# Three expert tiles instead of two from the routing of six batches, and the first one's layer 1 in four blocks between the steps of the last router

## The chip, the cores and the metric

The kernel runs on one NeuronCore of a Trainium2 chip: TensorE (PE; its weight loads are PEld), VectorE (DVE), ScalarE (ACT), GpSimd (POOL), the queues of the DMA engines, most of them fed by SyncE (SP), SBUF, and eight PSUM banks. The metric is device time in microseconds, the median of several runs. Every number of the profile comes from one profiled execution.

## The reference

Eight batches, eight heads, 1152 keys of 64 values. Queries are averaged in pairs, so each head has 576. After attention every one of the 8 x 576 = 4608 rows (512 values) goes to one of eight experts:

```python
q_pool = q.reshape(B, H, S // 2, 2, D).mean(axis=3)
attn = softmax(q_pool @ k.transpose(0, 1, 3, 2) / sqrt(D))
x = (attn @ v).transpose(0, 2, 1, 3).reshape(B * 576, 512)
logits = x @ w_gate                                  # 8 experts
e = argmax(logits, axis=1); gate = softmax(logits)[e]
eom = sigmoid(x @ w_output_gate)[e]
out = gate * eom * (relu(x @ w1[e]) @ w2[e])         # 512 -> 1024 -> 512
```

All is float32, and the kernel keeps that precision by splitting operands in a high and a low part.

## The kernel before, in words

**Attention.** The 32 pairs (batch, two heads) go through one software pipeline, written out by hand: 18 steps a pair (two heads, nine blocks of 128 keys), 576 steps and 14 more to empty it. In each step `sgen` issues the score products of one block (L395, L397) into one of two score areas of PSUM (`sps0`, `sps1`, two banks each), ACT makes the exponentials, and their low part `pl` comes from POOL (L411) or, in six steps of 18, from DVE (L405). `mgen` works a pair ahead on row maxima: products into one of three banks (`mp0` to `mp2`, handed out by `psum()`; `psum(True)` keeps a bank until `free`), and a DVE maximum of each (L333). `agen` runs six steps behind with P·V (L426 to L428), in bursts. `prep` loads and splits the next pairs.

**Router.** When a batch's four pairs are done, `logits` and `router` run as generators, moved on by one `yield` a step: transposes of the rows `xb` (L481), products with the gates (L498), sums in `lT` (L502), transposes of `lT` (L523), a chain of small DVE operations, and a product with a triangle (L555 to L558) that ranks each row within its expert. `cum` holds the counts so far. Five indirect DMAs from POOL write the row numbers to the list `idscr`, and the rows go to `xrows` in DRAM.

**Early experts.** After the sixth batch `setup` runs as part of that generator. It takes the counts of six batches, picks the expert with the most rows, takes 256 away, and picks again (so P1 = 2 tiles of 256 rows are full for certain before all is routed). It keeps its scratch in a held PSUM bank. Then `gather_ids` fetches both tiles' row numbers and `gather` the rows of the first.

**Expert tiles.** `Moe.run` handles two early tiles (t = -2, -1) and slots of 13 tiles of 256 rows, four of 192 and three of 128, whose experts and lists come from tables that DVE computes at run time (`totals1`, `totals2`, `table`, `fill`). For a tile, `xt` transposes the gathered rows and splits them into X; `l1` makes layer 1 in four blocks g (16 products each, L944), ACT and DVE add the parts and apply relu (`hs`, `hh`, `hl`); `l2` makes layer 2 for 128 rows at a time (L985 to L988). `split1` and `split2` make high and low parts of the weights: ACT casts, and DVE or POOL subtracts. Weights lie in two buffers, a and b, and `loads(t+2)` fills the one just used up. `gid` and `gat` gather a later tile's row numbers and rows; results are scattered to the output.

**Order at the join.** Orders of TensorE, DVE and ACT are written out within attention (there POOL too) and within the tiles; between these two, and for POOL and SP in the tiles, a scheduler with simulated times decides. `issue_after` and the list `behind` add pure order: in the kernel before, the transposes of tile -2 are pulled forward into the last P·V steps, block g = 0 of its layer 1 goes between the `lT` transposes and the rank product of the last router, and blocks 1 to 3 come after the rank product. SBUF is a stack: a tile of the expert part lies where one of attention lay, and waits for that one's last use.

## Time and profile before

| | us |
|---|---|
| median of three runs | 1492.92 |
| lowest and highest | 1492.88, 1496.63 |
| profiled execution | 1494.86 |
| its span | 1493.1 |
| granted TensorE clock, mean | 0.997 |
| DVE, ACT, POOL busy | 1104.3, 1124.7, 1025.1 |
| last score product starts | 1002.8 |
| last layer-2 product ends | 1486.7 |

Busy time of an engine counts its instructions, not its waits for semaphores. In a row of the time order, the number in brackets is the idle time before it, and the name behind the arrow is what ended it. In a row of the windows, each engine has its busy time and, in brackets, its instructions. Attention fills the first 1008 us, the expert tiles the rest.

### The profile page before, as it was taken

What the parts mean: (1) busy time and instruction counts of PE and PEld (TensorE: products, weight loads), DVE (VectorE), ACT (ScalarE), POOL (GpSimd) and SP (SyncE); (2) the same over time, 40 slices, a digit from 0 to 9 for tenths busy, and PEclk for the clock granted to TensorE, in tenths of its full rate; (3) what the DMA queues carried; (4) which work ended last, traced back from release to release, by engine and by line L of the source; (5) the groups of instructions that cost most, each with busy time, mean ns of one, the idle gap of its engine ahead of it and who ended that gap; (6) DMA issues with size and microseconds to landing.
All of it is one profiled execution on the core that took longest, in us unless ns stands there. A gap on an engine that the chain in (4) does not pass through costs nothing.

```text
span 1493.1 us, 40870 instructions
## 1 busy us (share of the span) xinstructions
PE 1461.7 (98%) x15806; PEld 1330.7 (89%) x15806; DVE 1104.3 (74%) x2374; ACT 1124.7 (75%) x1957; POOL 1025.1 (69%) x900
## 2 busy tenths in 40 slices
PE   7999999999999999999999999999999999999998
PEld 6999999999999999999999899987888888888985
DVE  7677777777777777777777777748888778777863
ACT  6888888888888888888888788884656556556662
POOL 5887889789889879888988898886533323333420
PEclk9999999999999999999999999999999999999999
DMA  5577567656567457755766555444966666666751
GB/s 172 147 179 193 134 157 175 169 136 166 146 163 189 124 137 170 177 148 130 178 168 162 152 136 146 112 147 136 374 244 232 232 240 213 240 234 231 263 211 63
DMA packets 96708, 265.97 MB, mean 178 GB/s; under 512 B 12826, under 2 KB 17066, under 8 KB 96498
## 3 DMA queue, kind: packets, MB, share of 16 engines
q1 hardware_dynamic: 85994, 241.52, 56.0%
q0 software_dynamic: 9088, 20.86, 4.0%
q8 instruction: 129, 2.11, 0.6%
q10 hardware_dynamic: 1424, 0.88, 0.2%
q14 instruction: 73, 0.60, 0.1%
HBM read 160.04 MB, written 22.50 MB: 122 GB/s over the span
## 4 chain that ended last, share of the span: by engine, by line
PE 92%; DVE 4%; DMA 1%; ACT 1%; issue 1%; POOL 1%; ACTq 0%; POOLq 0%; SPq 0%; DVEq 0%
PE mp L332 21%; PE hps L944 15%; PE sps L395 12%; PE sps L397 10%; PE av L426 6%; PE av L427 6%; PE av L428 6%; PE yp L985 4%; PE yp L986 4%; PE yp L988 4%; DVE pm L333 1%; PE tp L481 1%; PE tp L498 1%; PE xps L924 1%; PE yp L983 1%
## 5 line engine op out<-in xcount | busy, mean ns | idle before, releaser
L333 DVE TENSOR_REDUCE pm<-mp 128x1 f32<-128x384 f32 x864 | 452.8, 550 | 210.3 <-PE mp L332 209.5
L411 POOL TENSOR_TENSOR pl<-p,ph 128x576 f16<-128x576 f32 x386 | 493.8, 1285 | 135.0 <-ACT ph L410 103.4
L409 ACT ACTIVATE p<-sps 128x576 f32<-128x576 f32 x386 | 253.0, 655 | 88.7 <-PE sps L397 66.1
L332 PE MATMUL mp<-ka,qa 128*128 128x384 f32 x960 | 314.5, 344 | 0.8 <-DVE lT L502 0.6
L426 PEld LDWEIGHTS <-ph 128*128 128x128 f16 x2880 | 261.9, 96 | 39.4 <-issue 27.7
L426 PE MATMUL av<-vt,ph 128*128 128x65 f16 x2880 | 294.3, 193 | 0.0
L427 PE MATMUL av<-vt,ph 128*128 128x64 f16 x2880 | 292.3, 194 | 0.0
L428 PE MATMUL av<-vt,pl 128*128 128x65 f16 x2880 | 291.5, 192 | 0.0
L395 PE MATMUL sps<-qa,ka 128*128 128x288 f32 x1152 | 276.6, 321 | 4.3 <-DVE pl L405 3.4
L427 PEld LDWEIGHTS <-ph 128*128 128x128 f16 x2880 | 264.7, 97 | 0.8
L428 PEld LDWEIGHTS <-pl 128*128 128x128 f16 x2880 | 265.0, 99 | 0.0
L332 PE MATMUL mp<-kb,qb 66*128 66x384 f32 x768 | 260.4, 339 | 0.6 <-DVE kb L206 0.6
L410 ACT ACTIVATE ph<-sps 128x576 f16<-128x576 f32 x386 | 251.0, 650 | 0.0
L397 PE MATMUL sps<-qb,kb 68*128 68x288 f32 x1152 | 246.4, 296 | 1.0 <-DMA qb<-mr 1.0
L944 PE MATMUL hps<-x,w1h 128*128 128x512 f32 (+2 forms) x704 | 224.4, 382 | 0.6 <-DVE x L931 0.6
L395 PEld LDWEIGHTS sps<-qa,ka 128*128 128x128 f32 x1152 | 183.1, 190 | 7.3 <-DVE pl L405 1.9
L397 PEld LDWEIGHTS sps<-qb,kb 68*128 68x128 f32 x1152 | 185.0, 189 | 1.3 <-issue 1.2
L332 PEld LDWEIGHTS mp<-ka,qa 128*128 128x128 f32 x960 | 178.0, 190 | 3.1 <-DVE pm L333 2.0
L944 PE MATMUL hps<-x,w1l 128*128 128x256 f32 (+2 forms) x704 | 162.8, 272 | 0.0
L957 ACT COPY hs<-hps 128x512 f32<-128x512 f32 (+2 forms) x88 | 47.4, 539 | 147.9 <-PE hps L944 147.8
L405 DVE TENSOR_TENSOR pl<-sps,ph 128x576 f16<-128x576 f32 x190 | 143.6, 756 | 15.8 <-ACT sps L402 14.8
L401 ACT ACTIVATE ph<-sps 128x576 f16<-128x576 f32 x190 | 124.6, 656 | 38.1 <-PE sps L397 30.2
(271 smaller groups left out, 2948.1 us busy)
## 6 DMA issues: line engine op xcount, KB each, us to landing
ka<-xk SPq DMA_DIRECT2D x120, 288.0 KB
raw1a<-in_w_dram SPq DMA_DIRECT2D x22, 1024.0 KB
raw2a<-in_w_dram SPq DMA_DIRECT2D x22, 1024.0 KB
raw1b<-in_w_dram SPq DMA_DIRECT2D x22, 1024.0 KB
raw2b<-in_w_dram SPq DMA_DIRECT2D x22, 1024.0 KB
vp<-in_vL_dram SPq DMA_DIRECT2D x32, 576.0 KB
qp<-in_qT_dram SPq DMA_DIRECT2D x31, 576.0 KB
kpf<-in_kT_dram SPq DMA_DIRECT2D x31, 576.0 KB
```

The source lines that it names most:

```text
L332: nc.tensor.matmul(mp, lhsT=l, rhs=r, start=j == 0, stop=j == len(ops) - 1)
L333: nc.vector.tensor_reduce(out=pm[:, i:i + 1], in_=mp, axis=AX.X, op=ALU.max)
L395: nc.tensor.matmul(sps[:, j, 0:288], lhsT=ka[:, h, ks], rhs=qa[:, o + 288 * j:o + 288 * j + 288], start=True, stop=False)
L397: nc.tensor.matmul(sps[:, j, 0:288], lhsT=kb[:, h, ks], rhs=qb[:, h, 288 * j:288 * j + 288], start=False, stop=True)
L405: nc.vector.tensor_tensor(out=pl.rearrange("p (j n) -> p j n", j=2), in0=x, in1=ph2, op=ALU.subtract)
L409: nc.scalar.activation(out=p32.rearrange("p (j n) -> p j n", j=2), in_=x, func=AF.Exp, scale=1.0 / 16)
L410: e_ = nc.scalar.activation(out=ph2, in_=x, func=AF.Exp, scale=1.0 / 16)
L411: nc.gpsimd.tensor_tensor(out=pl, in0=p32, in1=ph, op=ALU.subtract)
L426: nc.tensor.matmul(av_[:, qb, 0:65], lhsT=hi, rhs=vt[:, h, c, 0:65], start=c == 0 and qb == 0, stop=False)
L427: nc.tensor.matmul(av_[:, qb, 0:64], lhsT=hi, rhs=vt[:, h, c, 66:130], start=False, stop=False)
L428: nc.tensor.matmul(av_[:, qb, 0:65], lhsT=lo, rhs=vt[:, h, c, 0:65], start=False, stop=c == NC - 1 and qb == 4)
L944: d['mm'] = nc.tensor.matmul(hp[:, f, 0:n], lhsT=W1[l][g][:, c, fs], rhs=d['x'][:, c, 0:n], start=c == 0 and l == 0, stop=c == 3 and l == 0)
```

## The change

P1 becomes 3, the slots of 256 rows 12, and tiles are numbered from -3. `setup` copies the counts out of PSUM at once, keeps its scratch in SBUF, and writes its scalar steps as `scalar_tensor_tensor` with a constant one; its gathers are issued one at a time, with three steps between them. The rows of tile -2 are gathered into a pool of their own (`me`), those of -1 into the common one. The stack has a new order: `vt` and `junk` get a pool of their own (`a_v`), X0 and the layer-1 sums (`mh`) move behind the low part of `w2`. The transposes of the first tile go before the first P·V product of the emptying steps (hook `pv`) and use the other score area, with one cast and one subtraction for all of X. Its layer 1 is cut into four blocks that stand behind the last P·V product, the last transposes of `xb`, the transposes of `lT` and the rank products; the hooks `xb`, `logit`, `rank` hold the router's next step back until a block is issued, `lg` and `r1` do the same on DVE with the block's sum. The first two parts of its `w2` are subtracted on POOL. The totals come after block four, and the tables are made in steps (`chain`) during tile -2; the third early tile's weights are loaded without a table.

```diff
-SLOTS = dict(D=13, T=4, S=3)
+SLOTS = dict(D=12, T=4, S=3)
 WIDTH = dict(D=256, T=192, S=128)
-DRAINS = (8, 17)
+DRAINS = (7, 16)
...
+        vp_ = pool("a_v", 1)
...
-                    nc.tensor.matmul(av_[:, qb, 0:65], lhsT=hi, rhs=vt[:, h, c, 0:65], start=c == 0 and qb == 0, stop=False)
+                    t_ = nc.tensor.matmul(av_[:, qb, 0:65], lhsT=hi, rhs=vt[:, h, c, 0:65], start=c == 0 and qb == 0, stop=False)
+                    if now[0] >= 18 * len(pairs):
+                        hooks.setdefault('pv', t_)
                     nc.tensor.matmul(av_[:, qb, 0:64], lhsT=hi, rhs=vt[:, h, c, 66:130], start=False, stop=False)
-                    nc.tensor.matmul(av_[:, qb, 0:65], lhsT=lo, rhs=vt[:, h, c, 0:65], start=False, stop=c == NC - 1 and qb == 4)
+                    hooks['av'] = nc.tensor.matmul(av_[:, qb, 0:65], lhsT=lo, rhs=vt[:, h, c, 0:65], start=False, stop=c == NC - 1 and qb == 4)
...
-                    nc.tensor.transpose(out=tx[:, 128 * i:128 * i + 128], in_=x, identity=ident)
+                    t_ = nc.tensor.transpose(out=tx[:, 128 * i:128 * i + 128], in_=x, identity=ident)
+                    hooks['xb' if c0 == 0 and i == 0 else 'xbl'] = t_
...
+                    if c0 == 0 and j == 0:
+                        hooks['logit'] = t_
...
-    def gather_ids(self, t, idx, pool, bufs):
+        self.hooks = {}
+
+    def ids_(self, t, idx, pool, bufs):
...
+            yield
...
-    def gather(self, t, pool, bufs, rows):
+    def rows_(self, t, pool, bufs, rows):
...
+            yield
...
         nc, kp, k, P1 = self.tc.nc, self.kp, self.keep, self.P1
         V = nc.vector
+        assert P1 == 3
         yield
         yield 1
-        cp, ck = psum(True)
+        cp = psum()
         nc.tensor.matmul(cp[:, 0:8], lhsT=k['ones'], rhs=self.cum, start=True, stop=True)
-        em = k['em8'][:, 0]
-        cn, eq, mx, mi, rb, ov = cp[:, 0:8], cp[:, 8:16], cp[:, 16:17], cp[:, 17:18], cp[:, 18:19], cp[:, 24:32]
+        em, one = k['em8'][:, 0], k['onesf'][:, 0:1]
+
+        def new(n, name, dt=F32):
+            return kp.tile([128, n], dt, name=name)
+        cn, eq, oh, mx, mi, ev, ov, rb = (new(n, x) for n, x in ((8, "cn"), (8, "eqe"), (8, "ohe"), (1, "mxe"), (1, "mie"), (1, "eve"), (1, "ove"), (2, "rbe")))
+        V.tensor_copy(out=cn, in_=cp[:, 0:8])
+        yield
         ris = []
-        V.memset(k['ef'][:, 0:2], 0.0)
-        V.memset(k['es'], 0)
         for i in range(P1):
-            oh = kp.tile([128, 8], F32, name=f"ohe{i}")
             V.tensor_reduce(out=mx, in_=cn, axis=AX.X, op=ALU.max)
-            yield
-            ms = kp.tile([128, 1], F32, name=f"mx{i}")
-            V.tensor_copy(out=ms, in_=mx)
-            V.tensor_tensor(out=eq, in0=cn, in1=ms.broadcast_to([128, 8]), op=ALU.is_equal)
+            V.tensor_tensor(out=eq, in0=cn, in1=mx.broadcast_to([128, 8]), op=ALU.is_equal)
             yield
             V.tensor_tensor(out=eq, in0=eq, in1=em, op=ALU.mult)
             V.tensor_reduce(out=mi, in_=eq, axis=AX.X, op=ALU.min)
             yield
-            V.tensor_scalar(out=k['ef'][:, i:i + 1], in0=mi, scalar1=8.0, scalar2=None, op0=ALU.add)
-            V.tensor_tensor(out=oh, in0=em, in1=mi.broadcast_to([128, 8]), op=ALU.is_equal)
-            yield
-            V.tensor_scalar(out=k['es'][:, i:i + 1], in0=mi, scalar1=8.0, scalar2=None, op0=ALU.add)
-            ri = kp.tile([128, 2], U32, name=f"ri{i}")
+            o = oh if i else k['oh1']
+            V.tensor_tensor(out=o, in0=em, in1=mi.broadcast_to([128, 8]), op=ALU.is_equal)
+            V.scalar_tensor_tensor(out=ev, in0=one, scalar=8.0, in1=mi, op0=ALU.mult, op1=ALU.add)
+            yield
+            if i >= P1 - 2:
+                V.scalar_tensor_tensor(out=k['ef'][:, i - P1 + 2:i - P1 + 3], in0=one, scalar=8.0, in1=mi, op0=ALU.mult, op1=ALU.add)
+            V.scalar_tensor_tensor(out=k['es'][:, i:i + 1], in0=one, scalar=8.0, in1=mi, op0=ALU.mult, op1=ALU.add)
+            if i < P1 - 1:
+                V.scalar_tensor_tensor(out=cn, in0=o, scalar=-float(TS), in1=cn, op0=ALU.mult, op1=ALU.add)
+            yield
+            ri = new(2, f"ri{i}", U32)
             ris.append(ri)
-            V.tensor_scalar(out=rb, in0=mi, scalar1=8.0, scalar2=float(ESTRIDE), op0=ALU.add, op1=ALU.mult)
+            V.scalar_tensor_tensor(out=rb if i else ri, in0=ev.broadcast_to([128, 2]), scalar=float(ESTRIDE), in1=k['Tp'][:, 0], op0=ALU.mult, op1=ALU.add)
+            yield
             if i:
-                V.tensor_tensor(out=ov, in0=oh, in1=k['oh1'], op=ALU.mult)
-                V.tensor_reduce(out=ms, in_=ov, axis=AX.X, op=ALU.add)
+                V.tensor_tensor(out=eq, in0=oh, in1=k['oh1'], op=ALU.mult)
+                V.tensor_reduce(out=ov, in_=eq, axis=AX.X, op=ALU.add)
                 yield
-                V.scalar_tensor_tensor(out=rb, in0=ms, scalar=float(TS), in1=rb, op0=ALU.mult, op1=ALU.add)
+                V.scalar_tensor_tensor(out=ri, in0=ov.broadcast_to([128, 2]), scalar=float(TS), in1=rb, op0=ALU.mult, op1=ALU.add)
                 V.tensor_tensor(out=k['oh1'], in0=k['oh1'], in1=oh, op=ALU.add)
-            else:
-                V.tensor_copy(out=k['oh1'], in_=oh)
-                if P1 > 1:
-                    V.scalar_tensor_tensor(out=cn, in0=oh, scalar=-float(TS), in1=cn, op0=ALU.mult, op1=ALU.add)
-            V.tensor_tensor(out=ri, in0=k['Tp'][:, 0], in1=rb.broadcast_to([128, 2]), op=ALU.add)
-            yield
-        free(ck)
-        yield
-        for i in range(P1):
-            self.gather_ids(i - P1, ris[i], kp, P1)
-            yield
-        for _ in range(8):
-            yield
-        self.gather(-P1, kp, 1, self.early)
+                yield
+
+        def apart(g):
+            for _ in g:
+                for _ in range(3):
+                    yield
+        yield from apart(self.ids_(-P1, ris[0], kp, P1))
+        yield from apart(self.rows_(-P1, kp, 1, self.early))
+        for i in range(1, P1):
+            yield from apart(self.ids_(i - P1, ris[i], kp, P1))
...
+            wq = pool("m_wq")
             mx = pool("m_x")
-            wq = pool("m_wq")
+            mh = pool("m_h")
+            me = pool("m_e")
...
+                    if t < 0:
+                        e = nc.sync.value_load(k['es'][0:1, t + P1:t + P1 + 1], min_val=0, max_val=7)
+                        lastw[0] = wload((t + P1) % 2, bass.ds(e, 1))
+                        return
...
-                xe = ps_h[1].tile([128, 2, 512], F32, name="hps") if t < -1 else None
+                xe = ps_h[0].tile([128, 2, 512], F32, name="hps") if t == -P1 else None
...
+                if xe is not None:
+                    z = xe.rearrange("p j (c n) -> p c j n", n=128)
+                    xv = x.rearrange("p c (l j n) -> p l c j n", l=2, n=128)
+                    fs = nc.scalar.copy(out=xv[:, 0], in_=z)
+                    V.tensor_tensor(out=xv[:, 1], in0=z, in1=xv.bitcast(F32)[:, 0], op=ALU.subtract)
+                    return fs, tr
...
-                hp = ps_h[g % 2].tile([128, 2, 512], F32, name="hps")
+                hp = ps_h[(g + 1) % 2].tile([128, 2, 512], F32, name="hps")
...
+            def chain():
+
+                totals2()
+                yield
+                yield from table('D', NT, z['nt'], TS, z['eo'], 2)
+                yield
                 fill('D', 0)
+                yield
+                gid(0)
+                gat(0)
+                yield
+                yield from totals2s()
...
+            def before(late, early):
+                tc.add_manual_dep(late.ins, early.ins.name, mybir.DependencyInfo(mybir.DependencyClass.NoSync, mybir.DependencyReason.DATA), reason="early tile in between")
+
+            def tile_(i, t, u):
 
                 acts = []
-                early = t < -1
+                head = t == -P1
+                d = T_[t]
                 for g in range(4):
-                    if halves(t) > 1 and not early:
+                    if halves(t) > 1 and not head:
                         with tc.issue_after(self.exps[-1]):
                             split2(t, g)
                     if acts:
                         acts.pop(0)()
                     if g == 0 and pend:
                         pend.pop(0)()
-                    if early and not pre:
-                        with tc.issue_after(self.behind[4]):
-                            pre.append(l1m(t, g))
-                    acts.append(l1(t, g, pre.pop(0) if pre else None))
-                    if early:
-                        if g == 1:
+                    if head:
+                        with tc.issue_after(hooks[('av', 'xbl', 'lt', 'ranked')[g]].ins):
+                            hp = l1m(t, g)
+                        acts.append(l1(t, g, hp))
+                        if g < 3:
+                            before(hooks[('xb', 'logit', 'rank')[g]], d['mm', g])
+                        if 0 < g < 3:
+                            before(hooks[(None, 'lg', 'r1')[g]], d['add', g])
+                        if g == 3:
                             totals1()
-                        with tc.issue_after(self.exps[-1]):
-                            split2(t, g)
+                        with tc.issue_after(self.exps[-2]):
+                            split2(t, g, nc.gpsimd if g < 2 else V)
+                    else:
+                        acts.append(l1(t, g))
                     if halves(t) == 1:
                         acts.pop(0)()
-                    if todo and not early:
-                        todo.pop(0)()
+                    if t == 1 - P1:
+                        next(late)
...
+                for c in (2, 3) if head else ():
+                    split1(u, c)
...
             pend = []
-            pre = []
             E = mybir.EngineType
-            for c in range(4):
-                with tc.issue_after(self.behind[1] if P1 > 1 and c == 3 else self.exps[-2]):
+            late = chain()
+            self.gather(1 - P1, me, 1, self.early)
+            with tc.issue_after(self.exps[-2]):
+                split1(order[0], 0, nc.gpsimd)
+            with tc.high_priority():
+                cast, tr = xt(order[0])
+            before(hooks['pv'], tr)
+            for c in range(1, 4):
+                with tc.issue_after(cast.ins):
                     split1(order[0], c, nc.gpsimd)
...
+            self.gather(2 - P1, mg, 3, self.early)
...
```

More of the change, by code (lines that the diff above doesn't have):

```diff
@@ L64, in make_lower, with attention @@
     nc.gpsimd.affine_select(out=tri, in_=tri, pattern=[[1, 128]], compare_op=ALU.is_gt, fill=0.0, base=0, channel_multiplier=-1)
-def attention(tc, qT, kT, vL, wg, keep, xrows, idscr, cum, pairs, setup, scat, init, exps, behind):
+def attention(tc, qT, kT, vL, wg, keep, xrows, idscr, cum, pairs, setup, scat, init, exps, hooks):
     nc = tc.nc
@@ L526, in router @@
             lh = sm.tile([128, 5, 16], F32, name="lg", bufs=2)
-            late = [V.tensor_copy(out=lh, in_=tv[:, :, 0:16])]
+            hooks['lg'] = V.tensor_copy(out=lh, in_=tv[:, :, 0:16])
             V.tensor_tensor(out=lg, in0=lh, in1=tv[:, :, 16:32], op=ALU.add)
@@ L537, in router @@
             V.tensor_tensor(out=eq, in0=g, in1=b8(mx), op=ALU.is_equal)
-            late.append(nc.scalar.activation(out=ex[:, :, 0:8], in_=ex[:, :, 0:8], func=AF.Exp))
+            nc.scalar.activation(out=ex[:, :, 0:8], in_=ex[:, :, 0:8], func=AF.Exp)
             e2 = sm.tile([128, 5, 8], F32, name="eq", bufs=2)
@@ L554, in router @@
             of = ohb.rearrange("p t e -> p (t e)")
-            late.append(nc.tensor.matmul(rk[:, 0:40], lhsT=tri, rhs=of, start=True, stop=False))
+            hooks['rank'] = nc.tensor.matmul(rk[:, 0:40], lhsT=tri, rhs=of, start=True, stop=False)
             for s_ in range(1, 5):
                 nc.tensor.matmul(rk[:, 8 * s_:40], lhsT=ones, rhs=of[:, 0:40 - 8 * s_], start=False, stop=False)
-            rl = nc.tensor.matmul(rv, lhsT=ones, rhs=cum.unsqueeze(1).broadcast_to([128, 5, 8]), start=False, stop=True)
-            if b == nb - 1:
-                behind.extend(i.ins for i in late + [lt, rl])
+            hooks['ranked'] = nc.tensor.matmul(rv, lhsT=ones, rhs=cum.unsqueeze(1).broadcast_to([128, 5, 8]), start=False, stop=True)
             sl = sm.tile([128, 5], F32, name="sl", bufs=2)
@@ L567, in router @@
             r1 = cut(rk, 40, 5, 8)
-            V.tensor_tensor(out=r1, in0=rv, in1=eoff, op=ALU.add)
+            hooks['r1'] = V.tensor_tensor(out=r1, in0=rv, in1=eoff, op=ALU.add)
             r2 = sm.tile([128, 5, 8], F32, name="r1", bufs=2)
@@ L725, in __init__ @@
         self.P1 = 0
-        while self.P1 < 2 and -(-(self.early - TS * self.P1) // 8) >= TS:
+        while self.P1 < 3 and -(-(self.early - TS * self.P1) // 8) >= TS:
             self.P1 += 1
@@ L760, in gather, with gather_ids @@
             self.T[t]['xg'].append(xg)
+            yield
+    def gather_ids(self, *args):
+        for _ in self.ids_(*args):
+            pass
+    def gather(self, *args):
+        for _ in self.rows_(*args):
+            pass
     def setup(self, psum, free):
@@ L911, in split2 @@
                 nc.scalar.copy(out=W2[0][:, z], in_=raw[:, z])
-                V.tensor_tensor(out=W2[1][:, z], in0=raw[:, z], in1=W2[0].bitcast(F32)[:, z], op=ALU.subtract)
+                eng.tensor_tensor(out=W2[1][:, z], in0=raw[:, z], in1=W2[0].bitcast(F32)[:, z], op=ALU.subtract)
             def xt(t):
@@ L955, in l1 @@
                 hh, hl = d['hh'][:, z, 0:w], d['hl'][:, z, 0:w]
-                hs = m1.tile([128, 2, TS], F32, name="hs", bufs=2)[:, :, 0:w]
+                hs = mh.tile([128, 2, TS], F32, name="hs", bufs=2)[:, :, 0:w]
                 nc.scalar.copy(out=hs, in_=hp[:, :, w:2 * w])
-                V.tensor_tensor(out=hs, in0=hp[:, :, 0:w], in1=hs, op=ALU.add)
+                d['add', g] = V.tensor_tensor(out=hs, in0=hp[:, :, 0:w], in1=hs, op=ALU.add)
                 def relu():
@@ L1008, in totals1 @@
             def totals1():
-                cp = z['cp'] = ps_y.tile([128, 512], F32, name="cp", tag="yp")
+                cp = ps_y.tile([128, 512], F32, name="cp", tag="yp")
                 nc.tensor.matmul(cp[:, 0:8], lhsT=k['ones'], rhs=self.cum, start=True, stop=True)
+                z['cp'] = m1.tile([128, 8], F32, name="cps")
+                V.tensor_copy(out=z['cp'], in_=cp[:, 0:8])
             def totals2():
@@ L1168, in ahead @@
                         loads(t + 2)
-                    gid(t + 3)
-                if not early:
+                    if not head:
+                        gid(t + 3)
+                if t != 1 - P1:
                     ahead()
@@ L1174, in tile_ @@
                         pack(t)
-                    if u is not None:
-                        split1(u, c, nc.gpsimd if early and c > 1 else V)
+                    if u is not None and not (head and c > 1):
+                        split1(u, c)
                     if acts:
                         acts.pop(0)()
-                    if not early:
+                    if not head:
                         next(late, None)
-                if early:
-                    todo.pop(0)()
+                if t == 1 - P1:
+                    ahead()
                 if u is not None and halves(t) == 1:
@@ L1187, in tile_ @@
                     loads(t + 2)
-                if not early:
+                if not head:
                     gat(t + 3)
@@ L1278, in body @@
         pairs = [(b, hp) for b in range(nb) for hp in range(4)]
-        attention(tc, qT, kT, vL, wg, keep, xrows, idscr, cum, pairs, m.setup, m.scat, init, m.exps, m.behind)
+        attention(tc, qT, kT, vL, wg, keep, xrows, idscr, cum, pairs, m.setup, m.scat, init, m.exps, m.hooks)
         m.run()
```

84 lines of the change are left out of this document (17 added, 67 removed).

## The prediction

> **What bounds the kernel now.** I read the busy line and the waits of the page first, then TensorE in order of time where attention ends and the expert tiles begin, then windows of equal work.
>
> ```profile
> span 1493.1 us, 40870 instructions
> PE 1461.7 (98%) x15806; PEld 1330.7 (89%) x15806; DVE 1104.3 (74%) x2374; ACT 1124.7 (75%) x1957; POOL 1025.1 (69%) x900
> L957 ACT COPY hs<-hps 128x512 f32<-128x512 f32 (+2 forms) x88 | 47.4, 539 | 147.9 <-PE hps L944 147.8
> ```
>
> TensorE is busy for 98%, so only its idle or slow time can be won: 31 us, start and end included. The 88 copies, four a tile, say 22 tiles. After the change there are 3+12+4+3 instead of 2+13+4+3, again 22: no arithmetic goes. The join looks like this on TensorE (idle before it and its releaser in brackets):
>
> ```profile
> 1005.34 1.09 PE L924 MATMUL hps<-ident,xg 128*128 128x128 f32 x8 [0.47 <-DVE pl L405]
> 1006.27 0.19 PE L426 MATMUL av<-vt,ph 128*128 128x65 f16 x1
> ...
> 1007.79 0.19 PE L428 MATMUL av<-vt,pl 128*128 128x65 f16 x1
> 1009.05 0.77 PE L481 MATMUL tp<-ident,xb 128*128 128x128 f32 x5 [1.07 <-DVE xb L437]
> 1013.05 0.80 PE L944 MATMUL hps<-x,w1h 128*128 128x512 f32 x1
> 1018.35 0.26 PE L555 MATMUL tp<-ohb,tri 128*128 128x40 bf16 x1
> 1033.64 0.66 PE L924 MATMUL xps<-ident,xg 128*128 128x128 f32 x4 [0.27 <-DMA xg<-xrows,ids]
> 1035.46 0.66 PE L924 MATMUL xps<-ident,xg 128*128 128x128 f32 x4 [1.16 <-DMA xg<-xrows,ids]
> 1060.01 0.66 PE L924 MATMUL xps<-ident,xg 128*128 128x128 f32 x4 [1.02 <-DMA xg<-xrows,ids]
> 1066.12 11.25 PE hps L944 x64
> ```
>
> The last P·V product ends at 1008.0. Then TensorE runs the last router alone until 1013.05, and one layer-1 block (of four) stands before the rank product at 1018.35. The last row, of the chain, is layer 1 undisturbed: 11.25 us, 2.81 a block. This one took 5.3. The windows say why (third column TensorE busy, then weight loads, DVE, ACT, POOL, granted clock, DMA share, GB/s):
>
> ```profile
> 1008.00:1013.00 5.00, 3.10 (x14) 1.95 (x14) 3.87 (x10) 1.84 (x5) 4.47 (x2) 0.90 1.03 397
> 1014.00:1016.00 2.00, 2.00 (x8) 1.71 (x7) 1.43 (x8) 1.38 (x3) 0.57 (x1) 0.50 0.77 286
> 1016.00:1018.00 2.00, 2.00 (x8) 1.71 (x7) 0.00 (x0) 0.00 (x0) 1.80 (x1) 0.50 0.03 12
> 1013.00:1027.34 14.34, 14.34 (x74) 12.14 (x72) 10.22 (x28) 7.77 (x12) 7.41 (x5) 0.80 0.50 154
> 1027.34:1041.48 14.14, 12.60 (x57) 9.48 (x56) 13.54 (x25) 8.08 (x10) 10.61 (x6) 1.00 0.15 39
> 1041.48:1066.12 24.64, 23.62 (x122) 19.84 (x122) 22.25 (x49) 13.43 (x18) 17.32 (x15) 1.00 0.83 315
> 1066.12:1089.15 23.03, 23.03 (x122) 19.66 (x121) 18.79 (x37) 13.22 (x18) 5.03 (x6) 1.00 0.93 351
> ```
>
> After the sparse 1008-1013 the clock is 0.50. A tile costs 23.03 us from 1066 on; so layer 2 with the next tile's transposes is 23.03 - 11.25 = 11.78. The second window from the end of layer 1 (14.14) holds 2.36 too much, the next tile (24.64) 1.61 too much: late row gathers.
>
> A second loss is in attention. Windows of one pair of heads each (36 of the score products of L397 in each):
>
> ```profile
> 699.50:729.62 30.12, 7.68 (x36) 5.78 (x37) 1.00 0.73 174
> 729.62:759.77 30.15, 7.70 (x36) 5.79 (x37) 1.00 0.60 160
> 821.73:856.54 34.81, 7.68 (x36) 5.80 (x37) 1.00 0.62 161
> 856.54:887.41 30.87, 7.70 (x36) 5.78 (x37) 1.00 0.51 124
> ```
>
> The third and fourth are the pairs in which `setup` picks the early experts; the first two stand at the same place of the batch before. Its price is 4.69 + 0.72 = 5.4 us.
>
> **The change, part by part: the join.** (a) The early transposes go before the last seven steps of P·V and write the score bank that is free first, and X0 moves to memory that is no longer P's. That ends the 0.47 wait: gain 0.5 (bounds 0 and 0.7).
>
> (b) Layer 1 of the first tile stands in four blocks: before the router's transposes, its logits, its rank product, and after it. From 1007.98 to the end of layer 1 at 1027.34 it is 19.36 now. After: 11.25 of blocks at full clock, 0.23 for the rank group (1018.35 to 1018.58), and 14 small router instructions. At the 0.12 of the early transposes (eight from 1005.34 to 1006.27) these are 1.6; the upper bound is the 3.10 busy of 1008-1013. To this come waits. The weights' low part is made on POOL:
>
> ```profile
> 1004.36 2.92 ACT L905 CAST w1h<-raw1a 128x1024 fp32r<-128x1024 f32 x3
> 1005.47 7.00 POOL L906 TENSOR_TENSOR w1l<-raw1a,w1h 128x1024 fp32r<-128x1024 f32 x3 [0.37 <-ACT w1h L905]
> ```
>
> 2.33 each. If ACT copies x first (two halves of 0.59 now, one whole after), the first w1l ends near 1004.4 + 1.1 + 1.0 + 2.4 = 1008.9 against a P·V end of about 1007.5: wait 1.4; if the weights go first, 0.3. I take 1.2, as x has priority. The copies of lT (two, some 0.45 each, no block between them and their transposes) cost 0.7. And `hl` on DVE, now amid POOL's weight work, may meet what these rows show:
>
> ```profile
> 1021.28 1.06 POOL L597 DMA_INDIRECT idscr<-tid,posi  x1 [3.48 <-DVE cum L592]
> 1033.36 2.13 DVE L1017 CAST nr<-ni 128x8 f32<-128x8 int32 x1
> 1035.53 2.32 DVE L1018 TENSOR_SCALAR ni<-ni 128x8 int32<-128x8 int32 x1
> 1033.02 4.79 POOL L906 TENSOR_TENSOR w1l<-raw1b,w1h 128x1024 fp32r<-128x1024 f32 x2
> ```
>
> Eight elements took as long as the POOL op beside them. One such wait in front of the router's work costs 0 to 2.3, two 4.7; I take 1.2, one in two. Sum 11.25 + 0.23 + 1.6 + 1.2 + 0.7 + 1.2 = 16.2: gain 3.2 (bounds -2.0, all upper ends, and 6.3, no waits).
>
> (c) The second tile's rows are gathered into a buffer of their own instead of behind the scatters (which begin at 1021.28, after `cum`). The 2.36 goes, but the totals product now waits behind block four for `cum`, which follows the sum of block three on DVE: 0.5, and DVE's last `hl` 0.5. Gain 1.4 (0 to 2.4). Two w2l parts go from DVE to POOL, 4.7 us at 2.33; with four w1l they end near 1005.5 + 14 = 1020, before the scatters are due, so they cost nothing there. Past that, each puts the scatters back by 2.3, for which only the rows of tile 0 wait, needed after two more tiles.
>
> (d) The tables run a tile earlier relative to their user, the third tile needs none: gain 1.6 (1.0 to 1.6). Its weight load is issued once w1l is done, beside a DMA share of 0.15; SP has only the last rows' write to order with it. The shifted drains keep their place in the order of tiles.
>
> The join: 0.5 + 3.2 + 1.4 + 1.6 = 6.7 (bounds -1.0 and 11.0).
>
> **The change: setup.** No PSUM bank is held through the picks any more, but a third pick comes and all its small operations read SBUF. Before, most had an operand in PSUM (L794 stands for them); three did not:
>
> ```profile
> L794 DVE TENSOR_SCALAR es<-tp 128x1 int32<-128x1 f32 x2 | 0.3, 150 | 0.0
> L803 DVE TENSOR_TENSOR oh<-oh,ohe 128x8 f32<-128x8 f32 x1 | 1.3, 1270 | 0.0
> L799 DVE TENSOR_TENSOR tp<-ohe,oh 128x8 f32<-128x8 f32 x1 | 1.0, 1018 | 0.0
> L805 DVE COPY oh<-ohe 128x8 f32<-128x8 f32 x1 | 0.9, 885 | 0.0
> L411 POOL TENSOR_TENSOR pl<-p,ph 128x576 f16<-128x576 f32 x386 | 493.8, 1285 | 135.0 <-ACT ph L410 103.4
> 565.41:626.90 61.49, 61.49 (x857) 58.65 (x854) 45.81 (x110) 53.20 (x99) 55.45 (x48) 1.00 0.67 166
> ```
>
> They waited for a POOL subtraction. After, 28 operations have two SBUF inputs: 13 tensor_tensor, 15 scalar_tensor_tensor. For the first kind L799 and L803 are the price. For the second, no row shows DVE waiting, but one shows POOL waiting for it: a gather's issue takes 997 ns in the median of 41, and 1.40 us beside an `hl`:
>
> ```profile
> L757 POOL DMA_INDIRECT xg<-xrows,ids x41: 991/997/1971, 881.8 to 1422.8; - x41
> 1031.44 0.68 DVE L965 SCALAR_TENSOR_TENSOR hl<-hs,hh 128x512 fp32r<-128x512 f32 x1
> 1031.61 1.40 POOL L757 DMA_INDIRECT xg<-xrows,ids  x1 [0.31 <-issue]
> ```
>
> The three picks take 19 steps, and a step is 30.12/18 = 1.67 us. DVE needs 45.81/61.49 of that, 1.25, in each, 23.6 in all, and 36 new operations at 0.17, 6.1. A wait is half a POOL op, 0.64, times POOL's busy share: 55.45/61.49 of 1.67 is 1.51 us a step, so 1.51/T for steps stretched to T. If all 28 wait, 19 T = 23.6 + 6.1 + 28 x 0.64 x 1.51/T = 29.7 + 27.0/T; T = 2.21, and 19 steps are 10.2 us too long. If only the 13 wait, T = 1.91: 4.5. I take 7, nearer the upper end for the POOL row, and not at it, since 1.51 also counts DMA issues, which hold DVE for less. Four more DMA issues on POOL, each 1.0 and now three steps apart, I cost at 0.3 (bounds 0 and 4): POOL's idle time, 6 us in 61.49, hides them. Setup: 7 + 0.3 - 5.4 = 1.9 lost (bounds 0.9 won and 8.8 lost).
>
> [...]
>
> Sum: -6.7 + 1.9 = -4.8. On the profiled execution (1494.86 us, span 1493.1) that is 1490.1; that execution lies 1.9 above the median of 1492.92, so **1488.1** for the median.
>
> **Rivals.** (1) Only the 13 wait: setup 4.5 + 0.3 - 5.4 = -0.6, time 1492.9 - 6.7 - 0.6 = 1485.6. For: no row shows a scalar_tensor_tensor delayed. Against: the POOL row. (2) Slower: in the two pairs of the picks each small operation waits a whole POOL op, as L1017 and L1018 did one after the other, because POOL starts its next op between two of them. Twice the wait: 19 T = 29.7 + 54/T, T = 2.64, 18.4 us; net 18.4 + 0.3 - 5.4 - 6.7 = +6.6, 1499.5. It turns the change into a loss once the picks cost 12 us. For: eight steps have two such operations. Against: POOL has gaps, one in ten of its time and more in a longer step. (3) The change doesn't do what it says: the second tile's gathers still come behind the scatters, landing near 1035 as now, and layer 2's second half waits about 5.5 us from 1030: 1493.6. For: POOL's order is a schedule's, not written out. Against: the buffer's memory, that of attention's loads, is free early. (4) The clock drops all the same, because the blocks leave gaps for w1l and lT: some 6.7 us at half speed as now (0.20 of 14.34, doubled, and one before 1013), 3.4 lost, 1491.5. For: it fell after 3.10 of 5.00 busy. Against: a block of 2.81 stands beside at most some 1.9 of waits and small work. (5) All 28 wait half a POOL op: the picks cost 10.2 instead of 7, 1491.3. For: L799, L803 and the POOL row. Against: DMA issues count in the 1.51.
>
> [...]
>
> **How the numbers follow.** Forecast 0.40, rivals in their order 0.17, 0.11, 0.10, 0.13, 0.09. A measurement here tells 0.3%, 4.5 us, from no change. The forecast, with 2.5 either way, is beyond that in 0.25 of its 0.40; (1) gives 0.16, (4) and (5) 0.03: faster 0.44. Slower: 0.10 of (2), 0.04 of (3) to (5): 0.14. Same 0.42. The range, 1483.5 to 1497.0, takes in (1), (3), (4), (5) and reaches towards (2); the forecast's own is 1485.6 to 1490.6.
>
> **What would show it.** Right: clock 1.00 throughout 1000-1040, no wait of the early transposes for xg, some 16 us from the last P·V to the end of the first layer 1, small operations of setup near 0.7 us in the mean, and the pairs of the picks together some 7 us longer than 60.3. Wrong: these operations at 0.17, a wait of the second tile's transposes for DMA, or a TensorE gap over 2 us between the blocks.

## The result, and the profile after

The changed kernel takes 1503.3 us (median of 6, 1499.6 to 1506.5) against 1493.9 for the kernel before beside it on the same chip: 1.0062 of its time, 95% interval 1.0042 to 1.0082. It is slower by 0.6%. Forecast were 1488.1 and a gain of 0.3%, and 1503.3 lies above the range, which ended at 1497.0. The profiled execution took 1502.7.

```profile
span 1501.0 us, 40878 instructions
```

The span grew by 7.9 us (1493.1 before). The same places as in the prediction, cut into windows (third column TensorE busy, then weight loads, DVE, ACT, POOL, granted clock, DMA share, GB/s):

```profile
1014.53:1029.90 15.37, 13.76 (x85) 11.43 (x84) 10.66 (x29) 9.10 (x16) 13.29 (x6) 1.00 0.97 359
1029.90:1046.33 16.43, 13.90 (x58) 11.28 (x59) 9.24 (x18) 6.78 (x9) 9.43 (x8) 0.90 0.90 242
1046.33:1070.66 24.33, 23.51 (x121) 19.55 (x121) 23.45 (x52) 14.51 (x20) 6.29 (x6) 1.00 0.17 56
...
1032.50:1036.30 3.80, 3.80 (x11) 2.95 (x12) 3.66 (x5) 1.44 (x2) 2.98 (x3) 0.58 1.08 255
```

TensorE in order of time at the join (start, duration; in brackets the idle time before it and its releaser):

```profile
1010.25 1.09 PE L936 MATMUL hps<-ident,xg 128*128 128x128 f32 x8
...
1014.34 0.19 PE L431 MATMUL av<-vt,pl 128*128 128x65 f16 x1
1014.81 0.50 PE L961 MATMUL hps<-x,w1h 128*128 128x512 f32 x1 [0.28 <-DVE x L942]
...
1023.04 0.76 PE L529 MATMUL tp<-ident,lT 32*128 32x32 f32 x5 [1.24 <-DVE lT L508]
...
1032.42 0.18 PE L1027 MATMUL cp<-cum,ones 128*128 128x8 bf16 x1 [2.52 <-DVE cum L596]
1032.46 0.48 PE L1002 MATMUL yp<-w2h,hh 128*128 128x512 f32 x1
```

And of the chain of waits, the layer 1 of three full tiles:

```profile
1070.66 11.20 PE hps L961 x64
1093.90 11.20 PE hps L961 x64
1117.16 11.20 PE hps L961 x64
```

Laid beside the windows of before, the 7.9 us split as follows. The last P·V ends at 1014.53 instead of 1007.98. Since neighbouring products overlap (the one at 1032.42 lasts 0.18, and the next begins at 1032.46), the inner cuts are good to 0.2 us.

| stretch | before | after | change | forecast |
|---|---|---|---|---|
| start to the end of the last P·V | 1007.98 | 1014.53 | +6.55 | +1.4 (setup +1.9, step (a) -0.5) |
| to the end of the first layer 1 (b) | 19.36 | 15.37 | -3.99 | -3.2 |
| to the next layer 1 (c) | 14.14 | 16.43 | +2.29 | -1.4 |
| to the one after that (d) | 24.64 | 24.33 | -0.31 | -1.6 |
| all further tiles, to the end of the span | 426.98 | 430.34 | +3.36 | 0 |

So the four blocks do what they were to do. Three other places lose: the picks, the wait for `cum`, and, nowhere in the prediction, every later tile: 23.26 us from one layer 1 to the next (1093.90 to 1117.16) where 23.03 stood before.

The two pairs of heads with the picks, as windows of 36 score products each (only these products are counted as busy):

```profile
822.22:862.06 39.84, 8.20 (x36) 6.30 (x36) 0.91 0.53 140
862.06:894.48 32.42, 7.70 (x36) 5.77 (x36) 1.00 0.53 139
```

72.3 us against an undisturbed 60.3: the picks cost 12.0 instead of 5.4. More than half of it is one instruction. DVE, POOL and TensorE around it:

```profile
837.89 7.50 DVE L795 TENSOR_TENSOR eqe<-cn,mxe 128x8 f32<-128x8 f32 x1
837.68 1.30 POOL L412 TENSOR_TENSOR pl<-p,ph 128x576 f16<-128x576 f32 x1
838.93 2.64 POOL L235 TENSOR_TENSOR kp<-kpf,xk 128x1152 fp32r<-128x1152 f32 x1
841.52 1.27 POOL L412 TENSOR_TENSOR pl<-p,ph 128x576 f16<-128x576 f32 x1
842.75 1.39 POOL L244 TENSOR_TENSOR yq<-yq,xq 128x576 fp32r<-128x576 f32 x1
844.11 1.26 POOL L412 TENSOR_TENSOR pl<-p,ph 128x576 f16<-128x576 f32 x1
845.32 0.52 POOL L249 CAST qd<-xq 64x64 fp32r<-64x64 f32 x2
845.92 0.69 PE L333 MATMUL mp<-ka,qa 128*128 128x384 f32 x1 [5.39 <-DVE pm L334]
```

An equality of eight elements began on DVE while POOL was in a subtraction, and ended when POOL went from its fifth subtraction in a row to a cast. The reductions queued behind it came late, TensorE stood for 5.4 us, and its clock, 0.50 from 846 to 852, was 0.91 over the pair.

### The profile page after: what moved, and what is told of

The parts are those of the page before. It is cut to its first block, busy times and chain, and to the rows that moved or that the text cites. A ratio compares the mean times of both kernels' runs of the same rounds, so it can differ in the third digit from the quotient of the medians.

```text
span 1501.0 us, 40878 instructions
## 1 busy us (share of the span) xinstructions
PE 1466.1 (98%) x15806; PEld 1332.6 (89%) x15806; DVE 1112.5 (74%) x2383; ACT 1125.6 (75%) x1956; POOL 1022.6 (68%) x900
## 4 chain that ended last, share of the span: by engine, by line
PE 91%; DVE 5%; ACT 2%; issue 1%; DMA 1%; ACTq 0%; POOL 0%; POOLq 0%; SPq 0%; DVEq 0%
PE mp L333 20%; PE hps L961 14%; PE sps L396 11%; PE sps L398 10%; PE av L427 6%; PE av L430 6%; PE av L431 5%; PE yp L1002 5%; PE yp L1003 5%; PE yp L1005 4%; DVE pm L334 2%; PE tp L484 1%; PE xps L936 1%; PE tp L502 1%; PE yp L1000 1%
```

## Experiments

Times are given as us over (or under) the kernel before run beside it; the kernel after stands at +9.5.

**The picks.** First, their rows and sums go back to a held PSUM bank (the steps, the third pick and the gathers stay):

```diff
-        cp = psum()
+        cp, ck = psum(True)
...
-        cn, eq, oh, mx, mi, ev, ov, rb = (new(n, x) for n, x in ...)
+        oh, mx, ov = (new(n, x) for n, x in ((8, "ohe"), (1, "mxe"), (1, "ove")))
+        cn, eq, oa, mi, ev, rb = cp[:, 0:8], cp[:, 8:16], cp[:, 16:24], cp[:, 24:25], cp[:, 25:26], cp[:, 26:28]
```

> The kernel after with one part undone: the three picks keep the count, the equality rows and the sums in a held PSUM bank, as the two picks of before did, so that no small operation reads two SBUF tensors; the steps and the gathers stay. (A pad keeps the expert buffers where they are in the kernel after.) Theory A (DVE waits for POOL): no small operation over 0.3 us, the 7.5 us of the first equality and TensorE's wait of 5.4 us are gone, and the two pairs of the picks cost some 3 to 5 us over 60.3 instead of 12; time 1494 to 1496. Theory B (the third pick's steps, or the gathers spread over steps, cost the time): the pairs stay above 70 us together, time 1501 to 1504.

+3.3 us (ratio 1.0025, 1.0016 to 1.0035), so 6.2 less than after. (The kernel also has the 32 bytes of `pad32` below, and keeps the sum of the picked experts in the bank until the end.) The pairs and two of the small operations:

```profile
821.46:855.34 33.88, 7.70 (x37) 5.80 (x38) 1.00 0.60 164
855.34:886.82 31.48, 7.70 (x37) 5.82 (x38) 1.00 0.55 143
```

```profile
L796 DVE TENSOR_TENSOR tp<-tp,mxe 128x8 f32<-128x8 f32 x3 | 0.5, 174 | 0.1
L798 DVE TENSOR_TENSOR tp<-tp,em 128x8 f32<-128x8 f32 x3 | 0.5, 165 | 0.0
```

The same equality took 0.17 us with one operand in PSUM, and no group of the picks' operations is above 0.174 in the mean. Theory A holds, though 1498.1 is 2 us above the time expected by it. What is left is 65.4 - 60.3 = 5.1 us without a single long operation. The held bank and the third pick's steps are there to cause it, and no run parts the two.

Second, SBUF rows as in after, but the picks wait out the stretch in which POOL works without a gap (835.06 to 845.37 in after):

```diff
         V.tensor_copy(out=cn, in_=cp[:, 0:8])
-        yield
+        for _ in range(6):
+            yield
...
         for i in range(P1):
+            for _ in range(6 if i == 2 else 0):
+                yield
```

> The kernel after with the picks paused for five steps ahead of the first equality and for six ahead of the third pick, so that their small operations fall where POOL does not work without a gap (it does so from 834.8 to 845.1 in the pair of the first pick); no operation is added or taken away. Theory A (an operation with two SBUF inputs can wait through several POOL operations in a row, and 7.5 us were such a run): no small operation takes over 1.4 us, TensorE's wait of 5.4 us is gone, the two or three pairs of the picks cost 4 to 7 us over 60.3 each two, instead of 12. Theory B (the first equality waits for something of its own, wherever it stands): it takes some 7 us again.

+3.1 us (1.0018, 1.0007 to 1.0029), 6.4 less than after, with no instruction taken away:

```profile
823.69:854.85 31.16, 7.81 (x36) 5.83 (x37) 1.00 0.67 179
854.86:886.53 31.67, 7.68 (x36) 5.77 (x37) 1.00 0.54 142
886.54:917.75 31.21, 7.69 (x36) 5.78 (x37) 1.00 0.59 143
```

The third pair, into which the third pick now falls, belongs to the price: 94.0 us for three pairs, 3.6 over undisturbed ones. The long wait belongs to the place, not to the operation: the three equalities took 0.30 us in the mean here. It is not a safe place, though: a later kernel with the same instructions here (the third of "all together", traced in the slowest of its eleven executions) had these rows, the second window and the group of the longest operation:

```profile
854.41:892.75 38.34, 7.95 (x37) 6.05 (x38) 0.91 0.45 117
```

```profile
L822 DVE TENSOR_TENSOR oh<-oh,ohe 128x8 f32<-128x8 f32 x1 | 2.7, 2668 | 0.0
```

**The tiles of 23.26 us.** Layer 2's products are what got slower. Groups of one kind between two equal places, of the kernel before, then of the one after:

```profile
L985 PE MATMUL yp<-w2h,hh 128*128 128x512 f32 x192 | 75.7, 394 | 0.0
L986 PE MATMUL yp<-w2l,hh 128*128 128x512 f32 x192 | 74.8, 389 | 0.0
...
L1002 PE MATMUL yp<-w2h,hh 128*128 128x512 f32 x192 | 77.1, 402 | 0.0
L1003 PE MATMUL yp<-w2l,hh 128*128 128x512 f32 x192 | 76.1, 396 | 0.0
```

Instructions, operands' shapes and waits are the same in both kernels, so I looked at where the buffers lie. First guess: all expert buffers of after begin 32 bytes off a multiple of 64, those of before on one.

```diff
     t('es', [128, 3], I32)
+    nc.vector.memset(t('pad', [128, 8], F32), 0.0)
```

> The kernel after with one more tile of 32 bytes a partition among the tiles kept throughout, so that every buffer of the expert part lies 32 bytes higher; no instruction but one clearing of that tile is added. Seen: a full tile takes 23.26 us after and 23.03 before, and the products of layer 2 follow one another at 0.233 us instead of 0.227, in all of some 14 full tiles. Theory A (the place): in the kernel after all these buffers begin 32 bytes off a multiple of 64, in the one before on one; moved by 32, a tile takes 23.03 again, and the whole is 3.3 us shorter than after (about 1500). Theory B (other traffic or another order of the work): the tile stays at 23.26 and the time at 1503.

> The kernel before with the same 32 bytes. Theory A (the place): a full tile takes 23.26 instead of 23.03, and the whole is 3.3 us longer than before (about 1497). Theory B: 23.03 and 1493.9 as before.

After with the pad: +10.5 us (1.0066, 1.0049 to 1.0083); before with the pad: +2.2 (1.0011, 1.0001 to 1.0021). The layer-1 rows of two tiles each, after with the pad, then before with it:

```profile
1097.66 11.20 PE hps L962 x64
1120.92 11.20 PE hps L962 x64
```

```profile
1095.82 11.25 PE hps L945 x64
1118.86 11.25 PE hps L945 x64
```

23.26 and 23.04: nothing moved with the place, in either. That theory fell (the 2.2 us of the second kernel are not in its tiles, and I did not trace them). The second guess is the distance between buffers. First the kernel before gets 64 bytes ahead of its weights, then the kernel after 960:

```diff
+            padm = pool("m_p").tile([128, 16], F32, name="padm")
+            V.memset(padm, 0.0)
             wa = pool("m_wa")
```

> A uniform shift of all buffers by 32 bytes changed nothing (tiles of 23.26 in the one kernel, 23.04 in the other). What also differs is where the buffers lie against each other: in the kernel before, hh, hl, x0, the parts of w1 and w2h begin at addresses that differ by multiples of 8192 bytes in a partition; in the one after, w1 and w2h lie 64 bytes beside such a multiple from hh and x0, since the second tile's rows got a pool of 4160 bytes below them. Here the kernel before gets a tile of 64 bytes in that place. Theory A (the distance between the operand that is loaded as weights and the one that streams sets the rate): a full tile takes 23.26 us instead of 23.03, layer 2 slower, layer 1 a little faster as in after, the whole 3.3 us longer than before. Theory B (the order of the work or its transfers): 23.03 and no change.

```diff
             me = pool("m_e")
+            mp_ = pool("m_p").tile([128, 240], F32, name="padm")
+            V.memset(mp_, 0.0)
```

> The kernel after with a tile of 960 bytes behind the second tile's rows, so that the distance is a multiple of 1024 bytes instead of 64 beside one. Theory A: if a multiple of 1024 is enough, a full tile takes 23.03 and the whole is 3.3 us shorter than after; if only larger multiples do it, between. Theory B: 23.26 and no change.

Before with 64 bytes: +4.3 us (1.0028, 1.0018 to 1.0038). Its rows, and those of after with 960 bytes:

```profile
1090.90 11.20 PE hps L946 x64
1114.17 11.20 PE hps L946 x64
```

```profile
1122.43 11.25 PE hps L963 x64
1145.47 11.25 PE hps L963 x64
```

Both swapped: 23.27 for before, 23.04 for after, layer 1 going the other way (11.20 with the 64 bytes, 11.25 without). So the place of `w1` and `w2h`, which these bytes move against `x`, `hh` and `w2l`, sets the rate, shown from both sides. It cannot be the distance between the two operands of each product alone: `w2l` and `hh` both lie ahead of the inserted bytes, nothing moved between them, and their products slowed too, 389 to 396. The time of after with 960 bytes did not fall (+10.5), and its trace says why: DVE stood 4.74 us ahead of the clearing of that tile, in the last pair of heads, released by POOL's operation on `vt` (L295); I take the tile to lie on memory that attention used until then. So the tile was set aside without being written:

> As the kernel with 960 bytes, but the tile is only set aside and never written: its clearing had waited 4.7 us on DVE for POOL in the last pair of heads and eaten the gain. Distance theory: a full tile 23.04 instead of 23.26, as seen, and the whole 3.3 us shorter than the kernel after (about 1500 where after has 1503.3). Rival: the clearing was not what ate it, and the time stays at 1503 or above.

+5.9 us (1.0044, 1.0027 to 1.0061), 3.6 less than after. From the same layer 1 (1069.54) to the end of the span it takes 427.2 us, against 430.3 in after and 427.0 in before. Its layer-2 groups, which answer to those above:

```profile
L1003 PE MATMUL yp<-w2h,hh 128*128 128x512 f32 x192 | 75.8, 395 | 0.0
...
L1004 PE MATMUL yp<-w2l,hh 128*128 128x512 f32 x192 | 74.8, 389 | 0.0
```

**The wait for `cum`.** In the kernel after, DVE works through this ahead of it:

```profile
1028.47 1.23 DVE L924 TENSOR_TENSOR w2l<-raw2a,w2h 128x1024 fp32r<-128x1024 f32 x1
...
1030.94 0.65 DVE L975 TENSOR_TENSOR hs<-hps,hs 128x512 f32<-128x512 f32 x1
...
1032.20 0.17 DVE L596 TENSOR_TENSOR cum<-tp,cum 128x8 bf16<-128x8 f32 x1
```

The first idea was to take the 1.23 out of its way:

```diff
-                            split2(t, g, nc.gpsimd if g < 2 else V)
+                            split2(t, g, nc.gpsimd if g < 3 else V)
```

> The kernel after with the third of the four w2l parts of the first tile on POOL as the first two are. Theory A (DVE's queue makes cum late): the 1.23 us go from DVE's queue ahead of cum, TensorE's wait of 2.5 us for cum falls to about 1.3, its clock is at 1.00 for more of 1032 to 1037; gain 1 to 3 us, time 1500 to 1502. Theory B (the router's own chain of small operations and round trips makes it late): the wait stays above 2.2 and the time at 1503.

+9.8 us (1.0063, 1.0047 to 1.0080), nothing won, and the wait grew to 2.88. DVE and POOL say why:

```profile
1031.27 2.48 DVE L982 SCALAR_TENSOR_TENSOR hl<-hs,hh 128x512 fp32r<-128x512 f32 x1
1030.78 2.41 POOL L924 TENSOR_TENSOR w2l<-raw2a,w2h 128x1024 fp32r<-128x1024 f32 x1 [0.70 <-ACT w2h L923]
```

The `hl` ahead of `cum`, 0.68 us in after and 2.48 here, now waits for the very work that was moved to POOL. Neither theory had that; it is the wait of the first equality again. Next, the totals product goes behind the first 24 products of layer 2, first in a bank of layer 1, then with its own buffer taken earlier:

```diff
-                        if g == 3:
-                            totals1()
...
                 pend.append(l2(t, 0))
+                if head:
+                    totals1()
```

> The kernel after with the totals product of cum behind the first 24 products of layer 2 of the first tile instead of ahead of them, in a free bank of layer 1. Theory A (TensorE's in-order wait of 2.5 us for cum is all that holds layer 2 up, and its slow clock from 1032.5 to 1036.3 follows from that wait): the wait is gone, layer 2 runs at 0.23 us a product from its start, and waits only some 1.0 us for the last hl; the next layer 1 begins 2.5 to 4 us earlier. Theory B (the operands of layer 2, w2l and hl, come as late as cum): the wait only moves to hl or w2l, and less than 1.5 us is won.

> The kernel after with the totals product behind the first 24 products of layer 2, and its PSUM buffer taken ahead of layer 2's, in the bank that the router's rank rows use until cum is done. In the first form of this layer 2 got that bank itself and waited 4.7 us for cum. Theory A (it is only TensorE's order and the bank): no wait for cum, layer 2 starts right behind layer 1 at full clock with some 0.7 us of waiting for the last hl; the start of the next layer 1 comes 16.7 - 3.5 = 13.2 us behind the end of the first one instead of 16.7 (from the start of the last product of the one to the first of the next); 3 to 3.5 us won, 1500. Theory B (layer 2's operands are late too): over 2 us of waits for w2l or hl appear there, and under 1.5 us is won.

Both lose: +12.4 (1.0086, 1.0069 to 1.0103) and +12.7 us (1.0090, 1.0074 to 1.0105). TensorE's waits of the first and of the second:

```profile
PE yp L1002 <- DVE cum L596: 4.7, 1, 4.7
```

```profile
PE yp L1002 <- DVE cum L596: 4.6, 1, 4.6
```

Layer 2 waits by itself now: in both programs its first half was given the PSUM bank that holds the router's rank rows until `cum` is read from them, and `cum` came later behind block four than in after (4.7 and 4.6 us of waiting instead of 2.52). So the expectation was tested by neither. The last form lets that half write a bank of layer 1:

```diff
+                if t == -P1 and j == 0:
+                    yp = ps_h[1].tile([128, 2, 512], F32, name="hps")[:, 0]
+                else:
+                    yp = ps_y.tile([128, 512], F32, name="yp", tag="yp")
```

> In both earlier forms layer 2's first half was still given the PSUM bank in which the router's rank rows lie until cum is done, so it waited 4.6 us for cum as before and the question stayed open. Here the first half of layer 2 of the first tile writes a bank of layer 1 that has been free since the third block, and the totals product comes behind it. Theory A (TensorE's wait for cum, by its order or by the bank, is what costs the first tile's layer 2 its time): no wait for cum, clock at 1.00 through layer 2, waits of 0 to 1.4 us for the last w2l and hl; from the start of the first tile's fourth block to the next layer 1 some 15.5 to 16.5 us instead of 19.3; 3 to 3.5 us won, 1500. Theory B (layer 2's own operands are as late): the wait moves to w2l or hl and stays over 2 us, under 1.5 us won.

+7.2 us (1.0053, 1.0038 to 1.0068), 2.3 less than after, where 3 to 3.5 were expected. Windows of the third block and of layer 2's start, and the longest wait:

```profile
1021.00:1026.00 5.00, 4.96 (x26) 4.16 (x26) 3.17 (x12) 0.87 (x2) 4.38 (x2) 0.66 0.91 367
1028.90:1036.00 7.10, 6.58 (x33) 4.99 (x32) 6.33 (x15) 3.95 (x5) 3.55 (x3) 1.00 0.86 228
```

```profile
PE hps L961 <- DVE x L949: 1.6, 1, 1.6
```

No wait for `cum`, and the clock is at 1.00 through layer 2: with the idle 2.5 us the slow clock behind it is gone. (In this execution it fell elsewhere, in the third block, behind the 1.24 us of lT: 0.66 in the first of these windows.) From the start of block four to the next layer 1 it takes 17.6 us instead of 19.3, not the 15.5 to 16.5 expected, since x of the second tile is late next, by 1.6 us.

**All together.** The three mends in one kernel, with the pauses and the second form of the totals; then with the last `hl` ahead of w1l; then with layer 2 in the free bank; then the same with the held bank in place of the pauses.

> All three mends together: picks paused while POOL works without a gap, layer 2 ahead of the totals product, and the distance of the operands at a multiple of 1024 bytes (a tile set aside, not written). If the three causes are what the change lost and they add: 1503.3 - 5.5 - 3.2 - 3.3 = 1491.3, some 0.2% faster than before (1494.9). If they overlap (a wait moves to another), between 1492 and 1497.

> The same, and DVE makes the last hl of the first tile ahead of the second tile's w1l part: the wait of layer 2 for hl (0.7 us) goes, 0.5 to 1.0 us less than without it; if w1l then comes late for the second tile's layer 1, no gain.

> The mends together, with layer 2 in the free bank: paused picks, distance a multiple of 1024, totals behind the first half of layer 2, the last hl ahead of the next w1l. If the causes add: the same with the wait of 4.6 for cum took 1494.2, of which some 5.5 to 6 go: 1488 to 1489, 0.3 to 0.4% faster than before. If the join's loss is elsewhere: 1493 to 1495.

> The same with the picks' rows in a held PSUM bank in place of the pauses. The held bank alone cost 5.1 us in the two pairs, without any wait of DVE for POOL; the pauses cost 2.6, 4.2 and 9.1 in three kernels with the same instructions there. If the held bank is the steadier price: 1488.5 to 1490, with less spread from execution to execution than with the pauses.

+0.8 us (1.0004, 0.9995 to 1.0013), +1.7 (1.0011, 1.0002 to 1.0020), -0.8 (0.9990, 0.9979 to 1.0002) and -3.2 (0.9982, 0.9972 to 0.9993; 1491.2 against 1494.5). The first two still had the wait for `cum`. For the last two, 1488 to 1489 and 1488.5 to 1490 were expected and 1493.7 and 1491.2 measured. The last is faster than both kernels of this case, by little. The single mends against after, -6.2 (held bank), -3.6 and -2.3, add to -12.1, which would leave -2.6; -3.2 was measured, with the earlier `hl`, which had won nothing in the second kernel. The sum fits, but loosely: the interval of after reaches 3 us to either side, those of the single mends 1.4 to 2.5. The three causes are shown one by one in their traces; that they are the whole loss is likely, not shown. The pauses made the third kernel's executions spread from 1490.3 to 1499.6, the held bank's from 1489.5 to 1494.3. What TensorE waits for next in the last kernel:

```profile
1036.79 0.50 PE L965 MATMUL hps<-x,w1h 128*128 128x512 f32 x1 [3.44 <-DVE x L953]
```

In its trace ACT's copy of that x is held until the last scatter of ids has landed (9.09 us idle, released by the DMA of `idscr`). What these 3.44 us would be worth was not tried.

## Why the prediction was wrong, point by point

**Setup: the term that was mis-sized most.** Forecast 7 + 0.3 against 5.4, a loss of 1.9; the two pairs lost 12.0 - 5.4 = 6.6, inside the term's own bound of 8.8 (the other 0.6 of the 7.2 at the start of the last pair lies outside these two). The wait itself was forecast rightly: of the operations with two SBUF inputs, the ten that took 0.64 us or more ended with a POOL operation, scalar_tensor_tensor too (L812's took 1.27 us), while the picks' reductions, with one input, took 0.14 to 0.16, that at 837.71 while POOL was in a subtraction. In before, L1017 and L1018, with one input, had taken 2.13 and 2.32, so the number of inputs alone does not part the operations that wait. What failed is the sentence "A wait is half a POOL op". Of the 28, 16 took 0.17 us or less, two 0.23 and 0.33, and nine 0.64 to 1.27, ending with the POOL operation beside them; but one, of 7.50, lasted through five: it waited on at four ends of POOL operations in a row (838.98, 841.57, 842.79 and 844.14). The mean over a uniform POOL left out that POOL has a long stretch without a gap in each of the two pairs (835.06 to 845.37 and 873.39 to 882.5), and that the wait of 7.50 us stopped TensorE for 5.39 and was followed by a clock of 0.50 from 846 to 852. Rival (2) had the point right from which it turns (picks at 12 us) and had given 0.11.

**(a)** held: no wait of the early transposes at 1010.25, and the delay of 7.2 us at the start of the last pair (979.39 to 986.61) is 6.55 at the end of the last P·V, 0.7 won, the term's upper bound.

**(b)** held, with the sum a little better than forecast: 15.37 instead of 16.2. Of its waits, `hl` amid POOL's weight work was 1.87 us against 0.68, the 1.2 forecast; w1l did not keep TensorE waiting at all (forecast 1.2), lT did for 1.24 (0.7). The `hl` and `lT` waits are one idle time here, since lT began on DVE (1022.58) as that `hl` ended (1020.78 and 1.87 long). So TensorE stood 1.6 us instead of 3.1, while its busy time was 13.76 instead of 13.08: two errors of the sum partly cancel, and that much of the hit is luck. The clock stayed at 1.00 through the blocks, so rival (4) did not come there; in one execution of another kernel, above, it did (0.66 from 1021 to 1026).

**(c)** has the wrong sign: +2.3 instead of -1.4. The gathers came in time (rival (3) fell: no wait for xg is left), but "the totals product now waits behind block four for `cum` ... 0.5" was 2.52. The step counted one DVE operation ahead of `cum`; between the rank product and `cum` DVE also makes a w2l part, an `hl` and two sums of blocks, in order. And the wait brought back the slow clock that (b) had removed: 0.58 over 3.8 us.

**(d)** gave 0.3 instead of 1.6. DVE is busy 23.45 of the 24.33 us of that tile: the tables now stand among w2l, w1l and `hl` of the same tile, and layer 2 waits 0.8 for an `hl`. Of the rest, 0.23 is the tile's own lengthening. No run tested this step alone, so that the tables cause that wait is not shown.

**The tiles behind the join** were taken as unchanged. The 4160 bytes for the second tile's rows moved w1 and w2h 64 bytes against x and `hh`, and the stretch lost 3.4 us, a term that the sum had at nothing. Nothing in the profile of before could show this, and I had put no cost on a buffer's place.

Of "what would show it", two points were wrong as they stand: the clock did not stay at 1.00 to 1040 (0.58 from 1032.5), and the pairs of the picks were 12 us longer, not 7. The small operations' mean came out at 0.71, as forecast, but by luck: without the one of 7.50 it is 0.46, and most stood at the 0.17 that was named as a sign of being wrong. The other points held; the TensorE gap of over 2 us came behind the last block, not between two.

## What to carry over

A mean wait of DVE for POOL, here 0.64 us times POOL's busy share, was a poor price where POOL works in a long unbroken run: look up the longest run at that place (835.06 to 845.37, 10.3 us, in which the equality took 7.50) as an estimate of the upper bound, and ask what stands behind the small operation. It is a bound and no forecast: in POOL's next long run (873.39 to 882.5) three operations of the picks took 0.78 to 1.25, each waiting for one POOL operation only. Before moving work between DVE and POOL, ask which DVE operation will then wait for it (`hl` went from 0.68 to 2.48 us). When a buffer is put between others, compare undisturbed stretches far from the edit too; if they moved, try the distance between the buffers before looking for a cause in the order of the work (64 bytes made 23.27 of 23.03 us).

## What the runs showed that I had not expected

Layer 2 of a tile, 48 products of 512 columns and eight transposes, takes 23.04 - 11.25 = 11.8 us when `w1` and `w2h` begin a multiple of 1024 bytes from x and `hh` in a partition, and 23.26 - 11.20 = 12.06 with 64 bytes more: 0.006 us a product. Layer 1 reacts the other way, by 0.05. Only distances of 0 and 64 bytes beside such a multiple were run, and the `w2l` products slow without a change of theirs, so the rule behind it stays open. The one shift of all buffers together was of 32 bytes; that a larger one would leave the rate alone is not shown. Between the two distances, 11.8 against 12.06, the place of the operands made 2 to 3% of layer 2.

TensorE's clock fell after 2.5 us without work (0.58 over the next 3.8), in the picks after 5.4 (0.50 over the next 6), and in one execution after 1.24 (0.66 over 5), where the same 1.24 left it at 1.00 in the kernel after. In before it was at 0.50 from 1012 to 1013, with no idle time above 1.07 ahead of it at the join. So the length of the last idle time alone does not tell whether it falls, and what does is not shown.

Why the equality at 837.89 waited on at four ends of POOL operations, and each of the nine that took 0.64 to 1.27 ended with the first, is not settled. TensorE's wait there was 5.3 to 5.5 us in every profile of a kernel with after's setup, so it is not chance.
